# Attention ahead of two expert layers: log series of the softmax sums on GpSimd, a cast and the log's first guess on ScalarE, pair 0 loaded over two queues, some constants set later

## The chip, the cores and the metric

One core of one Trainium2 chip runs one program. The metric is the device time of an execution in microseconds (us); lower is better. The core has TensorE (PE in the rows, its weight loads PEld), VectorE (DVE), ScalarE (ACT), GpSimd (POOL) and SyncE (SP), each with a queue of its own that runs in order, and 16 DMA engines that all queues feed. SP's rows are DMA issues.

## The reference

All inputs are float32. Attention has batch 4, 8 heads, 576 positions, head size 64:

```python
scores = scale * q @ k.T                       # scale = 1/8
cum = np.cumsum(np.log(np.clip(f, 1e-4, 1)), axis=-1)
scores = scores + cum[:, None] - cum[None, :]   # causal: the rest is -1e9
attn = np.exp(scores - max(scores))
attn = attn / (np.sum(attn) + 1e-9)
x = attn @ v                                   # to [2304, 512]
h = x @ w_in; x = np.maximum(0.01 * h, h) @ w_out
```

A layer of 8 experts follows: the tokens are dealt out by gate logits `x @ w_gate`, each expert takes 288 tokens through `max(x @ w1, 0) @ w2`.

## The kernel before, in words

The program has stages: attention (0 to about 213 us), the first half of the dense layer, its second half, the routing with what was deferred, and the experts. The change lies in attention and in constants at the top.

**Attention** runs over 16 pairs of heads. For each pair there are three groups of operations:

- `prepare` (line 606): loads k and q (`load`, `load_end`), transposes them on PE, and splits each into a high part (rounded, on ACT: kh, qh) and a low part (the rest, on DVE: kl, ql). Rows of negated running sums of log f come into `kr` by two DMAs from a DRAM buffer `cumd`.
- `offsets` (line 696): products of q and k with queries on the partitions (four matmuls a block, the last one with `kr`), the mask added and the row maximum taken on DVE (`kept`, `nm`), `exp` with row sums on ACT (`sm`). Then the log of the 10 columns of sums: `guess` (DVE: the float's bits times a constant), `ratio` (ACT: exp of the guess), `series` (DVE: six instructions on 128x10). `rows` (line 675) transposes the result on PE and puts it by two DMAs into the rows of `qr`.
- `attend` (line 788): the products again, now with keys on the partitions and `qr` as a last term, so that `exp` (ACT, into `P`) gives the finished weights; GpSimd zeroes the part above the diagonal; the product with v; `finish` (line 857) splits the result into high and low part (`xt`) and stores it. Half 0 (320 columns) has both parts on DVE, half 1 one on DVE and two steps on GpSimd (`FIN`, line 46).

Buffers: four sets of q/k tiles (`NS`), the set of pairs 0, 4, 8, 12 lies in the tile `X` and shows as X in the rows; four PSUM buffers `s` that all products share. The rows and columns of the sets that products read but no load writes are filled once by GpSimd memsets (`pads`, lines 586 to 600).

**The first expert weights** `wi0` (w_in, unpacked from pairs of 32-bit words) are made beside attention, 16 chunks: three DVE instructions on `wbits`, three GpSimd ones on `wsq` and `wst`, then per 1024 columns two ACT casts and two GpSimd subtractions into `wh`.

**The order.** `Plan` (line 91) is a list scheduler on the host: each operation has an engine, a cost in ns, needs, a rank and buffers; `order` lets each engine take the ready operation of lowest rank. What comes out is the order written into each engine's queue, and it does not change at run time. The ranks of a pair are 12 times its number plus the constants at the top: `ZP` prepare, `ZO` offsets, `ZA` attend, `ZH`/`ZL` high and low part, `ZS` blocks of attend, `ZT`, `ZR` the log, `ZN`/`ZM`/`ZB` offsets by pair; `ZW`, `DW`, `MW` date the weights. `MOVE` is its cost of a DMA.

At the top `make_identity`, the mask, `wgs` (gate weights, by a DMA on SP), `sel` (three DVE adds) and `wg2` are set up before attention; `wgs`, `sel` and `wg2` are first used in the dense stage.

Of the kernel before, what the change touches and what calls it, by code (L numbers as in the profile page):

```python
# [12 lines left out]
FT = mybir.dt.float32  # L13
# [36 lines left out]
NEAR = 11  # L50
NEARB = 5
ZN = 1, 0, 0, 0, 0, 0, 0, 0, 0, 0, 0, 0, 0, 0, 0, 1
ZM = -2.5, -0.5, 0, 0, 0, 0, 0, 0, 0, 0, 0, 0, 0, 0.5, 4, -4
ZB = 0, 0, -4, 0, 0, 0, 0, 0, 0, -2, 0, -4, 0, 0, 0, -1
# [5 lines left out]
PACE = 1.1  # L60

# [29 lines left out]
class Plan:  # L91
# [5 lines left out]
    MOVE = 650, 2200  # L97
# [27 lines left out]
    def order(self):  # L125
# [15 lines left out]
        def start(eng, t):  # L141
            nonlocal form
            q = ready.get(eng)
            while q and free.get(eng, 0) <= t:
# [16 lines left out]
                for b in o.takes:  # L161
                    r = taken[b.ring]
                    k = len(r) - self.depth[b.ring]
                    if k >= 0 and r[k].n:
                        blocked[b.ring].append(o)
                        break
                    if k >= 0 and max(x + self.hop(y, eng) for x, y in r[k].ends) > t:
                        post(max(x + self.hop(y, eng) for x, y in r[k].ends), "arrive", o)
                        break
                else:  # L170
                    for b in o.takes:
                        taken[b.ring].append(b)
# [12 lines left out]
                    free[eng] = t + ns + 25 * (eng == "sp")  # L185
                    done.append(o)
                    post(t + ns, "free", o)
                    if eng == "sp":
# [7 lines left out]
        while events:  # L196
# [3 lines left out]
            elif kind == "end":  # L200
                for u in o.users:
                    u.left -= 1
                    u.at = max(u.at, t + (self.MOVE[1] if o.eng == "sp" else self.hop(o.eng, u.eng)))
                    if not u.left:
                        post(u.at, "arrive", u)
                for b in o.uses:
                    b.n -= 1
                    b.ends.append((t + (self.MOVE[1] if o.eng == "sp" else 0), o.eng))
# [17 lines left out]
def tile_kernel(ctx, tc, q, k, v, f, w_in, w_out, w_gate, w1, w2, out):  # L226
# [14 lines left out]
    for w in WIDE1:  # L241
# [13 lines left out]
    G.affine_select(mask[:, 320:], mask[:, 320:], pattern=[[1, 128]], base=0, channel_multiplier=-1,  # L255
                    compare_op=OP.is_gt, fill=0.0)
# [118 lines left out]
    V.tensor_tensor(sel, sel, ident[:, 64:64 + E], op=OP.add)  # L375
    V.tensor_tensor(sel, sel, ident[:, 96:96 + E], op=OP.add)
    wg2 = cst.tile([128, 2 * NF, 32], FT, name="wg2")
    G.memset(wg2, 0.0)
# [142 lines left out]
    with ExitStack() as c1:  # L521
# [51 lines left out]
        cums = []  # L573
        for l in range(2):
            o = op("vec", 500, lambda l=l: negate(l), [o], -1000, (), [cb])
            cums.append(op("sp", 450, lambda l=l: sp.dma_start(cumd[l], pre["cn"][l].bitcast(FT)), [o], -1000, (), (), 200))
# [10 lines left out]
        for n in range(NS):  # L587
            i = n
            fs = [(560, lambda i=i: gp.memset(QR[i].bitcast(FT), 0.0)), (560, lambda i=i: gp.memset(KR[i].bitcast(FT), 0.0))]
            if n == 0:  # L590
                fs += [(150, lambda: gp.memset(QO.bitcast(FT), 0.0))]
                fs += [(150, lambda u=u: gp.memset(QO[64 * u:64 * u + 2].bitcast(FT), 1.0)) for u in range(2)]
            for u in range(2):
                fs += [(560, lambda i=i, u=u: gp.memset(QR[i][64 * u:64 * u + 2].bitcast(FT), 1.0)),
                       (560, lambda i=i, u=u: gp.memset(KR[i][64 * u + 32:64 * u + 34].bitcast(FT), 1.0))]
            for x, c in ((QH, 0), (QL, 0), (KH, S), (KL, S)):
                fs.append((100, lambda x=x[i], c=c: gp.memset(x[:, c:c + 64].bitcast(FT), 0.0)))
            if n < 2:
                fs.append((150, lambda n=n: gp.memset(VT[n][64:, 4], 0.0)))
            pads.append([op("gp", ns, fn, (), 12 * n - 100) for ns, fn in fs])  # L600


# [3 lines left out]
        def prepare(n, own, z):  # L606
# [5 lines left out]
            loads, buf = {}, {}  # L612

            def load(j, i):
# [4 lines left out]
                sp.dma_start(x3[j][:, :, i], src[b, h + i, :512].rearrange("(t p) d -> p t d", p=128))  # L619

            def load_end(j):
                if j == 0:
                    x3["end"] = at.tile([128, 2, D], FT, name="x4", tag="x4", bufs=2)
                sp.dma_start(x3["end"][64 * j:64 * j + 64], (q if j else k)[b, h:h + 2, 512:].rearrange("h p d -> p h d"))
            for j in range(2):
                o = op("sp", 450, lambda j=j: load(j, 0), (), z - 8, ["x3"], (), 728)
                buf[j] = o.got
                loads[j] = [o, op("sp", 450, lambda j=j: load(j, 1), [], z - 8, (), buf[j], 728)]
            o = op("sp", 625, lambda: load_end(0), (), z - 8, ["x4"], (), 182)
            buf["end"] = o.got  # L630
            loads["end"] = [o, op("sp", 625, lambda: load_end(1), [], z - 8, (), o.got, 182)]
# [38 lines left out]
            for u in range(2):  # L670
                outs[0].append(op("sp", 450, lambda u=u: sp.dma_start(kr[64 * u:64 * u + 2, :S].bitcast(FT), cumd[:, H * b + h + u]),
# [24 lines left out]
        def offsets(n, own, z):  # L696
# [70 lines left out]
            def guess():  # L767
                own["ln"] = x = at.tile([128, 3, 10], FT, name="ln", tag="ln", bufs=2)
                vec.tensor_scalar(x[:, 0], own["sm"].bitcast(I32), LN[0], LN[1], op0=OP.mult, op1=OP.add)

            def ratio():
                act.activation(own["ln"][:, 1], own["ln"][:, 0], AF.Exp)

            def series():
                x, t = own["ln"][:, 2], own["ln"][:, 1]
                vec.scalar_tensor_tensor(t, own["sm"], 1e-9, t, op0=OP.add, op1=OP.mult)
                vec.tensor_scalar(x, t, LN[5], LN[4], op0=OP.mult, op1=OP.add)
                vec.tensor_tensor(x, x, t, op=OP.mult)
                vec.scalar_tensor_tensor(x, x, LN[3], t, op0=OP.add, op1=OP.mult)
                vec.scalar_tensor_tensor(x, x, LN[2], own["ln"][:, 0], op0=OP.add, op1=OP.add)  # L780
                vec.tensor_tensor(x, x, own["nm"][:, :10], op=OP.add)
            o = op("vec", 80, guess, tots, z + ZR, ["ln"], [sb])
            lb = o.got[0]
            p = op("act", 230, ratio, [o], z + ZR, (), [lb])
            o = op("vec", 900, series, [p], z + ZR, (), [nb, sb, lb])
# [122 lines left out]
        run(plan)  # L908
        stp_.__exit__(None, None, None)
# [460 lines left out]
```

## Time and profile before

| | us |
|---|---|
| median of 3 runs (lowest, highest) | 941.02 (940.88, 943.09) |
| the profiled execution | 943.13 |
| its span, first to last instruction | 941.1 |
| PE busy in the span | 893.4 |
| DVE busy | 609.9 |
| ACT busy | 407.2 |
| POOL busy | 438.4 |

The profile is that of one execution. A busy time is the time in which an engine works on an instruction; matmuls are pipelined and their ends modelled, so PE's is rough. "Granted clock" is the share of TensorE's full speed that the chip gave. "x<-y" is what an instruction writes and reads, by tile names. A bracket such as [0.58 <-DVE nm L71] gives the idle time of the engine before an instruction and what ended it. Line L71 is the helper through which all planned operations pass, so rows are told apart by their tiles.

### The profile page before, as it was taken

What the parts mean: (1) busy time and instruction counts of PE and PEld (TensorE: products, weight loads), DVE (VectorE), ACT (ScalarE), POOL (GpSimd) and SP (SyncE); (2) the same over time, 40 slices, a digit from 0 to 9 for tenths busy, and PEclk for the clock granted to TensorE, in tenths of its full rate; (3) what the DMA queues carried; (4) which work ended last, traced back from release to release, by engine and by line L of the source; (5) the groups of instructions that cost most, each with busy time, mean ns of one, the idle gap of its engine ahead of it and who ended that gap; (6) DMA issues with size and microseconds to landing.
All of it is one profiled execution on the core that took longest, in us unless ns stands there. A gap on an engine that the chain in (4) does not pass through costs nothing.

```text
span 941.1 us, 19011 instructions
## 1 busy us (share of the span) xinstructions
PE 893.4 (95%) x6906; PEld 759.8 (81%) x6906; DVE 609.9 (65%) x1552; ACT 407.2 (43%) x949; POOL 438.4 (47%) x548
## 2 busy tenths in 40 slices
PE   6899899999999999999999999999959999999996
PEld 5688787887877887777777777777649999999996
DVE  6899999845789369523466766667735666566631
ACT  5988778861222223312222222123314555555521
POOL 8265666345999149100645655468752122221101
PEclk9999999999999999999899999999889999999998
DMA  5455565369985473521212221121336556556511
GB/s 130 105 156 157 143 161 141 95 196 294 334 298 173 156 222 117 178 90 45 85 62 69 68 68 49 65 68 49 116 126 192 175 187 193 191 185 204 182 41 33
DMA packets 139677, 131.81 MB, mean 140 GB/s; under 512 B 68448, under 2 KB 106656, under 8 KB 139584
## 3 DMA queue, kind: packets, MB, share of 16 engines
q1 hardware_dynamic: 136512, 121.17, 41.8%
q0 software_dynamic: 3072, 9.44, 3.4%
q8 instruction: 54, 0.88, 0.4%
q14 instruction: 39, 0.32, 0.1%
HBM read 99.85 MB, written 30.56 MB: 139 GB/s over the span
## 4 chain that ended last, share of the span: by engine, by line
PE 69%; DVE 11%; issue 11%; POOL 4%; ACT 3%; DMA 1%; POOLq 0%; SPq 0%; ACTq 0%; DVEq 0%
PE acc L1031 21%; PE h L71 21%; PE h L1087 7%; PE s L71 7%; PE y L1100 6%; PE T L71 3%; DVE kept L71 3%; DVE ln L71 3%; PE q_ct L1031 2%; DVE wbits L71 2%; ACT kept L71 2%; POOL out L1108 1%; DVE r_ge L1249 1%; DVE xt L71 1%; PE T L1077 1%
## 5 line engine op out<-in xcount | busy, mean ns | idle before, releaser
L71 PE MATMUL h<-X,wh 128*128 128x512 f32 (+1 forms) x960 | 211.1, 376 | 0.9 <-DVE g L71 0.9
L71 PEld LDWEIGHTS h<-X,wh 128*128 128x128 f32 x960 | 166.1, 189 | 38.4 <-DVE g L71 3.0
L1031 PE MATMUL acc<-wh,gh 128*128 128x512 f32 x576 | 190.3, 406 | 0.0
L461 POOL TENSOR_TENSOR gl<-g,gh 128x512 fp32r<-128x512 f32 x64 | 104.1, 1631 | 75.5 <-ACT gh L460 72.3
L1031 PEld LDWEIGHTS acc<-wh,gh 128*128 128x128 f32 x576 | 108.8, 193 | 19.5
L1087 PE MATMUL h<-XE,wh 128*128 128x288 f32 x768 | 118.3, 303 | 0.3 <-ACT XE L1078 0.3
L71 DVE TENSOR_TENSOR wh<-wst,wh 128x512 fp32r<-128x512 f32 x132 | 90.5, 707 | 42.8 <-ACT wh L360 31.2
L1031 PE MATMUL acc<-wh,gl 128*128 128x512 f32 x288 | 116.9, 406 | 0.0
L360 ACT CAST wh<-wst 128x512 fp32r<-128x512 f32 x132 | 80.4, 621 | 79.9 <-DMA wst<-in_moe_w 47.2
L1087 PEld LDWEIGHTS h<-XE,wh 128*128 128x128 f32 x768 | 106.5, 191 | 0.6 <-ACT XE L1078 0.6
L460 ACT CAST gh<-g 128x512 fp32r<-128x512 f32 x64 | 39.5, 621 | 141.6 <-PE acc L1031 127.1
L71 ACT ACTIVATE g<-h 128x512 f32<-128x512 f32 (+1 forms) x72 | 39.5, 551 | 139.0 <-PE h L71 136.8
L1100 PE MATMUL y<-eh,wh 128*128 128x288 f32 x512 | 98.4, 296 | 0.0
L71 ACT ACTIVATE kept<-kept,nm 128x192 f32<-128x192 f32 (+4 forms) x160 | 87.8, 551 | 17.1 <-DVE nm L71 16.9
L1108 POOL DMA_INDIRECT out<-yo,ids x24 | 24.7, 1028 | 129.3 <-DVE yo L1107 120.1
L1100 PEld LDWEIGHTS y<-eh,wh 128*128 128x128 f32 x512 | 79.5, 188 | 0.2 <-ACT eh L1091 0.2
L71 DVE TENSOR_TENSOR g<-g,h 128x512 f32<-128x512 f32 (+1 forms) x72 | 44.6, 621 | 51.9 <-ACT g L71 51.9
L71 DVE SCALAR_TENSOR_TENSOR wbits<-w,wbits 128x256 int32<-128x256 int32 x128 | 75.3, 589 | 2.8
L71 POOL TENSOR_TENSOR wst<-wsq,wbits 128x256 f32<-128x256 f32 x64 | 49.8, 779 | 46.4 <-DVE wbits L71 42.3
L1100 PE MATMUL y<-el,wh 128*128 128x288 f32 x256 | 67.9, 296 | 0.0
L1031 PEld LDWEIGHTS acc<-wh,gl 128*128 128x128 f32 x288 | 55.4, 192 | 9.8
L71 POOL TENSOR_SCALAR wsq<-wsq 128x256 f32<-128x256 f32 x64 | 59.9, 935 | 5.6
(210 smaller groups left out, 1605.3 us busy)
## 6 DMA issues: line engine op xcount, KB each, us to landing
wst<-in_moe_w SPq DMA_DIRECT2D x128, 256.0 KB
X<-xd SPq DMA_DIRECT2D x12, 1024.0 KB
g<-gd SPq DMA_DIRECT2D x36, 256.0 KB
w<-in_moe_w_in SPq DMA_DIRECT2D x32, 256.0 KB
w<-in_moe_w_out SPq DMA_DIRECT2D x32, 256.0 KB
gd<-g SPq DMA_DIRECT2D x16, 512.0 KB
xd<-xt SPq DMA_DIRECT2D x16, 320.0 KB
x2d<-xo SPq DMA_DIRECT2D x18, 256.0 KB
```

Source lines behind the costliest of these rows:

```text
L71: r = getattr(self.engine, name)(*a, **k)
L360: A.copy(r[u][0], x)
L460: A.copy(gh, g)
L461: G.tensor_tensor(gl, g, gh, op=OP.subtract)
L1031: tc.keep_in_program_order(PE.matmul(*a, **k))
L1077: PE.transpose(p[:, M * t:M * t + M], xe[t][:, 128 * c:128 * c + 128], ident[:M, :M])
L1087: PE.matmul(h[:, :CAP], w, X[:, c, x, :], start=n == 0, stop=n == 3 * NC - 1)
L1100: PE.matmul(yt[c][:, :CAP], w[:, s], a, start=j == 0 and n == 0, stop=j == NJ - 1 and n == 2)
L1108: sd = G.indirect_dma_start(out=out[:, :], out_offset=bass.IndirectOffsetOnAxis(ap=ids[:, 3 * e + t:3 * e + t + 1], axis=0), in_=y, in_off ...
L1249: V.scalar_tensor_tensor(many[:, :NT * (K + 1)].rearrange("p (i k) -> p i k", k=K + 1)[:, :, :K], key[:, :, None].to_broadcast(s), base if ...
```

## The change

- `guess` is dropped on DVE; `ratio` makes it on ACT (copy with scale and bias of the sums' bits) ahead of the exp. The series runs on GpSimd, in nine instructions (`ready` and `series`) in place of six.
- The high part of half 0 is cast on ACT (`FIN`).
- Pair 0: q is loaded from ACT's queue (a planner engine "aq"), its rows of running sums come straight from SBUF (`pre["cn"]`) instead of through `cumd`, and its three `KR` memsets go to DVE. The small pads come before the long ones.
- The mask's triangle, `wgs`, `sel` and `wg2` move back, the last three behind the attention plan.
- Ranks, weight dates, `NEAR` and the planner's DMA cost change.

```diff
-ZP, ZO, ZA, ZH, ZL, ZW, DW = -38, -27, 5, -6, -14.5, 68.5, 15.5
-ZS = 7, 3.5, 7, 1, 3.5, 11.5, 15.5
+ZP, ZO, ZA, ZH, ZL, ZW, DW = -39, -27, 5, -9.5, -10.5, 63, 14.5
+ZS = 5, 5.5, 7, 0.5, 2.5, 11, 11.5
-ZT = -4, 5.5
-ZR = 5
-MW = 2.5, 0.65
+ZT = 0, 7
+ZR = 5.5
+MW = 1.5, 0.6
-FIN = ("vec", "vec"), ("vec", "gp")
+FIN = ("act", "vec"), ("vec", "gp")
-NEAR = 11
+NEAR = 10
...
-    MOVE = 650, 2200
+    MOVE = 650, 2600
...
-    G.affine_select(mask[:, 320:], mask[:, 320:], ...)
...
-    G.memset(wgs, 0.0)
-    with nc.allow_non_contiguous_dma(reason="small"):
-        nc.sync.dma_start(wgs[:, :, :E], w_gate.rearrange("(c p) e -> p c e", p=128))
-    V.tensor_tensor(sel, ident[:, 0:E], ident[:, 32:32 + E], op=OP.add)
...
-    G.memset(wg2, 0.0)
...
+            on = (vec, "vec") if n == 0 else (gp, "gp")
...
+            for x, c in ((KH, S), (KL, S), (QH, 0), (QL, 0)):
                 fs.append((100, lambda x=x[i], c=c: gp.memset(x[:, c:c + 64].bitcast(FT), 0.0)))
+            fs.append((570, lambda i=i: gp.memset(QR[i].bitcast(FT), 0.0)))
+            fs += [(670, lambda i=i, u=u: gp.memset(QR[i][64 * u:64 * u + 2].bitcast(FT), 1.0)) for u in range(2)]
+            ks = [(570, lambda i=i, e=on[0]: e.memset(KR[i].bitcast(FT), 0.0))]
+            ks += [(670, lambda i=i, u=u, e=on[0]: e.memset(KR[i][64 * u + 32:64 * u + 34].bitcast(FT), 1.0)) for u in range(2)]
+            pads.append([op(on[1], ns, fn, (), 12 * n - (100 if n else 1001)) for ns, fn in ks] + [op("gp", ns, fn, (), 12 * n - 100) for ns, fn in fs])
...
+            at_q = (sp, act) if n == 0 else (sp, sp)
+            on = ("sp", "aq") if n == 0 else ("sp", "sp")
...
-                sp.dma_start(x3[j][:, :, i], src[b, h + i, :512].rearrange("(t p) d -> p t d", p=128))
+                at_q[j].dma_start(x3[j][:, :, i], src[b, h + i, :512].rearrange("(t p) d -> p t d", p=128))
...
+                if n == 0:
+                    outs[0].append(op("sp", 450, lambda l=u: sp.dma_start(kr[l:l + 65:64, :S].bitcast(FT), pre["cn"][l][:2].bitcast(FT)), [negs[u]] + pads[0], z + 1, (), [sets[0]], 30))
+                    continue
...
-            def guess():
-                own["ln"] = x = at.tile([128, 3, 10], FT, name="ln", tag="ln", bufs=2)
-                vec.tensor_scalar(x[:, 0], own["sm"].bitcast(I32), LN[0], LN[1], op0=OP.mult, op1=OP.add)
             def ratio():
-                act.activation(own["ln"][:, 1], own["ln"][:, 0], AF.Exp)
+                own["ln"] = x = at.tile([128, 4, 10], FT, name="ln", tag="ln", bufs=2)
+                act.activation(x[:, 0], own["sm"].bitcast(I32), AF.Copy, scale=LN[0], bias=LN[1])
+                act.activation(x[:, 1], x[:, 0], AF.Exp)
+            def ready():
+                x = own["ln"]
+                gp.tensor_scalar(x[:, 3], own["sm"], 1e-9, None, op0=OP.add)
             def series():
                 x, t = own["ln"][:, 2], own["ln"][:, 1]
-                vec.scalar_tensor_tensor(t, own["sm"], 1e-9, t, op0=OP.add, op1=OP.mult)
-                vec.tensor_scalar(x, t, LN[5], LN[4], op0=OP.mult, op1=OP.add)
...
+                gp.tensor_tensor(t, own["ln"][:, 3], t, op=OP.mult)
+                gp.tensor_scalar(x, t, LN[5], LN[4], op0=OP.mult, op1=OP.add)
+                gp.tensor_tensor(x, x, t, op=OP.mult)
+                gp.tensor_scalar(x, x, LN[3], None, op0=OP.add)
+                gp.tensor_tensor(x, x, t, op=OP.mult)
+                gp.tensor_scalar(x, x, LN[2], None, op0=OP.add)
+                gp.tensor_tensor(x, x, own["ln"][:, 0], op=OP.add)
+                gp.tensor_tensor(x, x, own["nm"][:, :10], op=OP.add)
+            o = op("act", 450, ratio, tots, z + ZR, ["ln"], [sb])
+            p = op("gp", 250, ready, tots + [o], z + ZR, (), [sb, lb])
+            o = op("gp", 2200, series, [o, p], z + ZR, (), [nb, sb, lb])
...
         run(plan)
+        G.memset(wgs, 0.0)
+        with nc.allow_non_contiguous_dma(reason="small"):
+            nc.sync.dma_start(wgs[:, :, :E], w_gate.rearrange("(c p) e -> p c e", p=128))
+        V.tensor_tensor(sel, ident[:, 0:E], ident[:, 32:32 + E], op=OP.add)
...
+        G.memset(wg2, 0.0)
```

## Rows read from the trace of the kernel before

**Rows 1.** Stretch view: stretch, length, busy PE, PEld, DVE, ACT, POOL, clock, DMA.
```profile
45.00:165.00 120.00, 110.14 (x1319) 96.47 (x1317) 110.73 (x408) 99.32 (x292) 76.16 (x117) 0.99 0.57 151
```

**Rows 2.** Timeline of PE (start, us): transposed rows, and scores of pair 8.
```profile
55.24 0.27 PE L71 MATMUL s<-ident,ln 128*10 128x128 f32 x1 [0.58 <-DVE nm L71]
...
117.72 0.28 PE L71 MATMUL s<-ident,ln 128*10 128x128 f32 x1 [0.58 <-DVE nm L71]
...
134.47 2.67 PE L71 MATMUL s<-X 64*128 64x320 f32 x32
...
156.39 0.27 PE L71 MATMUL s<-ident,ln 128*10 128x128 f32 x1
...
190.78 0.28 PE L71 MATMUL s<-ident,ln 128*10 128x128 f32 x1
```

**Rows 3.** Waits of PE, 15 to 195 us: total, times, longest.
```profile
PE s L71 <- DVE nm L71: 11.0, 20, 2.0
```

**Rows 4.** Timeline of PE, the longest of these waits.
```profile
142.86 0.40 PE L71 MATMUL s<-kh,qh 64*128 64x288 f32 x2 [1.96 <-DVE nm L71]
```

**Rows 5.** Stretch view just after that wait, columns as in rows 1.
```profile
144.00:146.00 2.00, 1.76 (x8) 1.58 (x9) 2.00 (x14) 2.00 (x7) 1.31 (x3) 0.50 0.00 0
```

**Rows 6.** Timeline of all engines at the front.
```profile
0.79 1.28 ACT L71 ACT_TABLE_LOAD   x1 [0.79 <-PEq L1357]
...
1.25 0.41 SPq L372 DMA_DIRECT2D wgs<-in_moe_w_gate  x1
...
1.71 1.06 SPq L71 DMA_DIRECT2D x<-in_k  x2
...
2.81 1.06 SPq L71 DMA_DIRECT2D x<-in_q  x2
...
3.58 0.68 ACT L71 ACTIVATE ft<-ft 32x576 f32<-32x576 f32 x1 [1.50 <-DVE ft L71]
...
6.42 0.75 DVE L71 SCALAR_TENSOR_TENSOR kept<-cum,kept 32x576 fp32r<-32x576 f32 x1
...
11.17 0.59 SPq L71 DMA_DIRECT2D X<-cumd  x2
...
11.85 0.16 POOL L71 MEMSET kl<- 128x64 f32 x1
...
13.01 0.93 PE L71 MATMUL s<-X,qo 64*128 64x192 f32 x2 [0.18 <-POOL qr L71]
```

**Rows 7.** Stretch view of the ln tile alone: busy PE, PEld, DVE, ACT, clock, DMA.
```profile
0.00:215.00 215.00, 4.50 (x16) 1.36 (x16) 35.54 (x112) 3.34 (x16) 0.98 0.53 142
```

**Rows 8.** The ln tile by instruction: ns min/median/max, 0 to 215 us.
```profile
L71 DVE SCALAR_TENSOR_TENSOR ln<-ln x32: 169/314/1295, 25.2 to 195.9; 128x10 f32<-128x10 f32 x32
```

**Rows 9.** Timeline of DVE and POOL at 112 us.
```profile
111.99 2.54 POOL L71 TENSOR_TENSOR wh<-wst,wh 128x512 fp32r<-128x512 f32 x2
112.01 2.54 DVE L71 SCALAR_TENSOR_TENSOR ln<-ln 128x10 f32<-128x10 f32 x2
```

**Rows 10.** Groups of instructions, POOL, whole span: count | busy us, mean ns.
```profile
L1298 POOL TENSOR_SCALAR r_nr<-r_rp 128x8 f32<-128x8 f32 x7 | 2.2, 319 | 2.4 <-DVE r_rp L1282 2.0
...
L1300 POOL TENSOR_TENSOR r_nr<-r_nr,r_r 128x8 f32<-128x8 f32 x7 | 1.7, 236 | 0.5
```

**Rows 11.** Groups of instructions, ACT, 0 to 215 us.
```profile
L71 ACT CAST kh<-s 128x512 fp32r<-128x512 f32 x12 | 6.8, 564 | 3.4 <-PE s L71 3.4
...
L71 ACT ACTIVATE ln<-ln 128x10 f32<-128x10 f32 x16 | 3.3, 209 | 8.1 <-DVE ln L71 8.1
...
L71 ACT CAST kh<-s 128x64 fp32r<-128x64 f32 x12 | 2.3, 191 | 0.0
```

**Rows 12.** The xt tile by instruction, 0 to 215 us.
```profile
L71 DVE CAST xt<-s x16: 474/479/493, 46.2 to 211.8; 128x320 fp32r<-128x320 f32 x16
```

**Rows 13.** Timeline of SP and POOL at the stage's end.
```profile
213.29 2.99 SPq L71 DMA_DIRECT2D w<-in_moe_w_out  x4
...
215.04 0.74 POOL L71 TENSOR_TENSOR xt<-xt 128x256 fp32r<-128x256 f32 x1
```

More of the change, by code (lines that the diff above doesn't have):

```diff
@@ L49 @@
 WIDE2 = (0,), (1, 2), (3, 4), (5, 6), (7, 8)
-NEAR = 11
+NEAR = 10
 NEARB = 5
-ZN = 1, 0, 0, 0, 0, 0, 0, 0, 0, 0, 0, 0, 0, 0, 0, 1
-ZM = -2.5, -0.5, 0, 0, 0, 0, 0, 0, 0, 0, 0, 0, 0, 0.5, 4, -4
-ZB = 0, 0, -4, 0, 0, 0, 0, 0, 0, -2, 0, -4, 0, 0, 0, -1
+ZN = 0.5, 0, -4, 0, 0, 0, -0.5, 0, 0, 0, 0, 0, 0, 0, 2, 0.5
+ZM = -2.5, -0.5, 0, -1, 0, 0, 0, 0, 0, 0, 0, 1, -1.5, 0.5, 4, -4
+ZB = 0, -4, -5, 0, 0, 0.5, -0.5, 0, 0, -3, 0, -4, 0.5, 0, 0, -1
 NK = 4
@@ L60 @@
 PACE = 1.1
+QS = "sp", "aq"
 class InOrder:
@@ L184, in start @@
                         form = o.form
-                    free[eng] = t + ns + 25 * (eng == "sp")
+                    free[eng] = t + ns + 25 * (eng in QS)
                     done.append(o)
                     post(t + ns, "free", o)
-                    if eng == "sp":
+                    if eng in QS:
                         free["dma"] = max(free.get("dma", 0), t + ns + self.MOVE[0]) + o.move
@@ L202, in order @@
                     u.left -= 1
-                    u.at = max(u.at, t + (self.MOVE[1] if o.eng == "sp" else self.hop(o.eng, u.eng)))
+                    u.at = max(u.at, t + (self.MOVE[1] if o.eng in QS else self.hop(o.eng, u.eng)))
                     if not u.left:
@@ L207, in order @@
                     b.n -= 1
-                    b.ends.append((t + (self.MOVE[1] if o.eng == "sp" else 0), o.eng))
+                    b.ends.append((t + (self.MOVE[1] if o.eng in QS else 0), o.eng))
                     if not b.n:
@@ L254, in tile_kernel @@
     V.memset(mask[:, 320:], -1e9)
-    G.affine_select(mask[:, 320:], mask[:, 320:], pattern=[[1, 128]], base=0, channel_multiplier=-1,
-                    compare_op=OP.is_gt, fill=0.0)
     ones = cst.tile([128, 32], FT, name="ones")
@@ L572, in tile_kernel @@
         cb = o.got[0]
-        cums = []
+        cums, negs = [], []
         for l in range(2):
             o = op("vec", 500, lambda l=l: negate(l), [o], -1000, (), [cb])
+            negs.append(o)
             cums.append(op("sp", 450, lambda l=l: sp.dma_start(cumd[l], pre["cn"][l].bitcast(FT)), [o], -1000, (), (), 200))
@@ L588, in tile_kernel @@
             i = n
-            fs = [(560, lambda i=i: gp.memset(QR[i].bitcast(FT), 0.0)), (560, lambda i=i: gp.memset(KR[i].bitcast(FT), 0.0))]
+            on = (vec, "vec") if n == 0 else (gp, "gp")
+            fs = []
             if n == 0:
                 fs += [(150, lambda: gp.memset(QO.bitcast(FT), 0.0))]
[L592 to L596, printed above, removed]
-                fs.append((100, lambda x=x[i], c=c: gp.memset(x[:, c:c + 64].bitcast(FT), 0.0)))
+                fs += [(220, lambda u=u: gp.memset(QO[64 * u:64 * u + 2].bitcast(FT), 1.0)) for u in range(2)]
+            for x, c in ((KH, S), (KL, S), (QH, 0), (QL, 0)):
+                fs.append((100, lambda x=x[i], c=c: gp.memset(x[:, c:c + 64].bitcast(FT), 0.0)))
+            fs.append((570, lambda i=i: gp.memset(QR[i].bitcast(FT), 0.0)))
[4 more added lines that the diff above has]
+            if n == 0:
+                op("gp", 470, lambda: gp.affine_select(mask[:, 320:], mask[:, 320:], pattern=[[1, 128]], base=0, channel_multiplier=-1,
+                                                       compare_op=OP.is_gt, fill=0.0), (), -99)
             if n < 2:
-                fs.append((150, lambda n=n: gp.memset(VT[n][64:, 4], 0.0)))
-            pads.append([op("gp", ns, fn, (), 12 * n - 100) for ns, fn in fs])
+                op("gp", 150, lambda n=n: gp.memset(VT[n][64:, 4], 0.0), (), 12 * n - 90)
         marks, users = [], []
@@ L623, in load_end @@
                     x3["end"] = at.tile([128, 2, D], FT, name="x4", tag="x4", bufs=2)
-                sp.dma_start(x3["end"][64 * j:64 * j + 64], (q if j else k)[b, h:h + 2, 512:].rearrange("h p d -> p h d"))
+                at_q[j].dma_start(x3["end"][64 * j:64 * j + 64], (q if j else k)[b, h:h + 2, 512:].rearrange("h p d -> p h d"))
             for j in range(2):
-                o = op("sp", 450, lambda j=j: load(j, 0), (), z - 8, ["x3"], (), 728)
+                o = op(on[j], 450, lambda j=j: load(j, 0), (), z - 8, ["x3"], (), 728)
                 buf[j] = o.got
-                loads[j] = [o, op("sp", 450, lambda j=j: load(j, 1), [], z - 8, (), buf[j], 728)]
+                loads[j] = [o, op(on[j], 450, lambda j=j: load(j, 1), [], z - 8, (), buf[j], 728)]
             o = op("sp", 625, lambda: load_end(0), (), z - 8, ["x4"], (), 182)
             buf["end"] = o.got
-            loads["end"] = [o, op("sp", 625, lambda: load_end(1), [], z - 8, (), o.got, 182)]
+            loads["end"] = [o, op(on[1], 625, lambda: load_end(1), [], z - 8, (), o.got, 182)]
             sets = {}
@@ L908, in tile_kernel @@
         run(plan)
+        G.memset(wgs, 0.0)
+        with nc.allow_non_contiguous_dma(reason="small"):
+            nc.sync.dma_start(wgs[:, :, :E], w_gate.rearrange("(c p) e -> p c e", p=128))
+        V.tensor_tensor(sel, ident[:, 0:E], ident[:, 32:32 + E], op=OP.add)
+        V.tensor_tensor(sel, sel, ident[:, 64:64 + E], op=OP.add)
+        V.tensor_tensor(sel, sel, ident[:, 96:96 + E], op=OP.add)
+        G.memset(wg2, 0.0)
         stp_.__exit__(None, None, None)
```

10 lines of the change are left out of this document (1 added, 9 removed).

## The prediction
> **What bounds the kernel now.** The busy times by stretch come first: in the attention stage, from 45 to 165 us, TensorE (PE) is busy 110.14 and VectorE (DVE) 110.73 of 120 us, ScalarE (ACT) 99.32, GpSimd (POOL) 76.16 [rows 1]. Two engines stand at 92%, so an average does not say which one sets the pace. The order of time does: PE transposes the log-sum rows of each head pair once, and the starts of these 16 transpositions are the clock of the stage. From 55.24 to 156.39 us there are 8 intervals of 12.64 us, from 156.39 to 190.78 three of 11.46 [rows 2]. The slow intervals are those in which DVE and POOL also unpack the first expert weights. PE does the same work in both, so 1.18 us of each slow interval is not PE's. The waits say whose it is: between 15 and 195 us PE waited 11.0 us for DVE's row maxima, in 20 waits [rows 3]. One such wait (1.96 us) ends at 142.86 us, and the granted clock from 144 to 146 us is 0.50, the 1.2 GHz level instead of 2.4 [rows 4, 5]; PE had stood idle just before. So DVE's queue sets the slow intervals, and PE the rest.
>
> Before 13 us another chain holds: the first scores need zeroed pads, and the pads end on POOL at about 12.0 us; their last product needs the running sums of f, whose way through DRAM ends at 13.01 us [rows 6].
>
> **The log series leaves DVE.** On DVE the ln instructions take 35.54 us in all, 2.22 us a pair [rows 7]. That is mostly not work: 32 of them have a median of 314 ns and a minimum of 169 [rows 8], and at 112.01 us two took 2.54 us together while POOL ran two weight subtractions over the same 2.54 us [rows 9]. POOL gets nine small instructions a pair instead. The nearest rows are 128x8 ones of the routing stage, 319 ns for a scalar form and 236 for a two-tensor form [rows 10]: four and five of these are 4 x 0.319 + 5 x 0.236 = 2.46 us. POOL has 76.16/120 x 12.64 = 8.02 us an interval now, so 10.5 after. ACT computes the guess: one more instruction like its ln one, 0.21 us [rows 11]. The page "SBUF — State Buffer" of the Trainium skill, section "SBUF: two separate sides", states that DVE and GpSimd share a port pair by an exclusive lock: a DVE instruction with two SBUF inputs and a GpSimd one that reads SBUF do not run together, and the later waits out the earlier. The pair at 112.01 us agrees; it speaks against this change as well, since nine more POOL instructions meet the weight unpacking that stays on DVE. What that would cost is a rival below.
>
> **Half of the rounding leaves DVE.** The 320-wide cast takes 479 ns on DVE [rows 12]. On ACT it lies between the 64- and 512-wide casts, 191 and 564 ns [rows 11]: 0.40 us by width. DVE is relieved by 2.22 + 0.48 = 2.70 us a pair, ACT gets 0.61 more: from 99.32/120 x 12.64 = 10.46 to 11.07 us an interval.
>
> **What this is worth.** With DVE 2.7 us below its 11.66 us an interval (110.73/120 x 12.64), PE's 11.46 is the floor, with ACT at 11.07 and POOL at 10.5 close under it. The bounds of the gain are 0 and 1.18 us an interval; in-order queues this full will not reach the floor, so I take two thirds, 0.8, nearer to the floor because most of PE's waiting is put down to DVE. 8 x 0.8 = 6.4 us. Outside the 8 intervals I take nothing.
> The new guess and series make the chain from sums to rows about 0.45 us longer (2.46 + 0.21 + 0.21 against 2.22 + 0.21). It is covered: the rows transposed at 117.72 us belong to pair 8 (the ninth), whose scores start at 134.47 [rows 2], 16.7 us later. If that cover were gone the price would be 0.45 x 16 = 7 us. What is not covered is PE's own queue: the transposition stands between other PE work, and everything behind it waits when the series is late. The new ranks of the planner (ZS, ZT, ZH, ZL, ZR, the three lists by pair, the weight dates and the longer DMA allowance) cost no instruction; they only move work, and I price them inside the 0 to 1.18.
>
> **The front.** The DMA of the gate weights leaves SP's queue in front of the first k load: issue 0.41 us, so k starts at 1.25 instead of 1.71 us [rows 6]. The q loads of pair 0, issued at 2.81 us now, go to ACT's queue; even behind ACT's table load (0.79 + 1.28 = 2.07 us) they are issued 0.7 us earlier [rows 6]. They cost ACT three issues, ahead of its logarithm of f, before which it waits 1.50 us today [rows 6]. PE's first transpositions move up by about 0.5 us with the loads. On POOL the pads of pair 0 now precede the long memsets, three memsets go to DVE, and the constants go behind the stage; pads then end before 7 us and no longer decide. The running sums are ready on DVE at 6.42 + 0.75 = 7.17 us. Today they go to DRAM and come back: read back from 11.17 us, used at 13.01, 1.84 us from issue to use [rows 6]. Going straight from SBUF, an issue at 7.3 us gives a use at about 9.2. DVE's three memsets of about 0.6 us each fill its idle time ahead of f; should f wait for them, 0.4 us is lost. I take 13.01 - 9.2 - 0.4 = 3.4 us. Bounds: 4.3 if the way is still shorter; 0.5 if the next wait, the loads of pair 1 through the same SP queue, leaves only the wgs issue. If this cover fails the later pairs start as now.
>
> **The end.** The weights' first loads are issued on SP at 213.29 us, and POOL's last attention instruction runs from 215.04 to 215.78 [rows 13]. The gate weights' memset and DMA now stand behind the stage. If they are put in front of those loads, SP adds 0.41 us of issue, and at worst waits for POOL until 215.78: 2.5 us. I take 0.4 and keep 0 to 2.9. The selector's three DVE instructions and the second memset of POOL land in a stretch where both engines wait for these loads.
>
> **Sum.** -6.4 - 3.4 + 0.4 = -9.4 us. The profiled execution took 943.13 us (span 941.1), the median of the three runs is 941.02, 0.2% less; the difference is carried to the median: 931.6 us, given as 931.5.
>
> **Rivals.**
> *Only the front pays.* ACT or PE takes the place of DVE at once: ACT at 11.07 us an interval has to wait for PE and DVE in turn, and the interval stays 12.6. For it: ACT is third at 83% and gets work. Against it: PE's listed waits are for DVE. Time: 941.0 - 3.4 + 0.4 = 938.0 us.
> *The floor is reached.* All 8 intervals go to 11.46 us, the front gives 4.3, and the three intervals before 55.24 us give some 0.5 each: 9.4 + 4.3 + 1.5 = 15.2, so 926 us. For it: DVE would have slack everywhere. Against: ACT and POOL stand within 1 us of PE.
> *Slower: GpSimd delivers the rows late.* The series waits in POOL's queue behind weight work; a block like the one at 111.99 us is 2.54 us long [rows 9]. If it stands behind half such a block in each of the 8 intervals, PE's transposition and all PE work behind it wait 1.27 us: +10.2 us, no relief, -3.4 + 0.4 for front and end: 948 us. It decides once PE waits more than about 1.2 us a pair for POOL. For it: POOL goes to 10.5 of 12.6 us an interval, and the weights' dates are pulled earlier (MW), which packs POOL further. Against it: POOL now waits much of its time, and 16.7 us lie between rows and their use. By the port lock of the Trainium skill's page above, half of the nine instructions waiting out a DVE one of 0.31 us would be an estimated 1.4 us a pair, 941.0 + 8 x 1.4 - 3.0 = 949 us: the same rival by another cause. No row here shows small POOL instructions beside DVE.
>
> **How the numbers follow.** Forecast (927 to 936): 0.47. Only the front (936 to 941): 0.26, a little over half of it below the border. The floor (below 927): 0.13. Slower: 0.14. A measurement of this kernel can tell about 0.3%, 2.8 us, from no change, so faster means below 938.2. Faster 0.47 + 0.13 + 0.14 = 0.74, same 0.12, slower 0.14. The range runs from 924, just past the floor, to 942, which takes in the front case with its worst end (938.0 + 2.5 = 940.5) and leaves out the slower rival.
>
> **What would show it.** Right: the intervals between row transpositions in the weight stretch fall to about 11.8 us, PE's waits for DVE's maxima fall under half of 11.0 us, DVE's busy time there falls below 80% with ACT above 90%, and the product that now waits until 13.01 us goes at 9 to 10. Wrong: PE waits before the row transposition with POOL's ln as releaser (the slower rival); intervals that stay at 12.6 with ACT waited for (only the front); a first product still near 13 us; or w_out loads issued 2 us or more behind the last attention product.

## The result and the profile after

The changed kernel takes 930.4 us (median of 4 runs, 928.31 to 931.35); the kernel before, run beside it, 942.06 (4 runs, 940.88 to 943.10). The ratio is 0.987, 95% interval 0.986 to 0.989. The forecast was 931.5 us with a range of 924 to 942. The profiled execution took 930.69 us, its span 929.0, against 943.13 and 941.1.

The same stretch of the attention stage as in [rows 1]: stretch, length, then busy us (instructions) of PE, PEld, DVE, ACT and POOL, granted clock, DMA share, GB/s.

```profile
45.00:165.00 120.00, 117.55 (x1455) 103.28 (x1451) 87.88 (x355) 113.87 (x339) 97.53 (x219) 1.00 0.59 155
```

DVE fell from 110.73 to 87.88 us, PE rose from 110.14 to 117.55, the clock from 0.99 to 1.00. ACT is at 95% now, POOL at 81%. PE's timeline, the transpositions of the log-sum rows, to be read against [rows 2] (start, length):

```profile
36.33 0.28 PE L72 MATMUL s<-ident,ln 128*10 128x128 f32 x1 [0.55 <-POOL ln L72]
53.74 0.28 PE L72 MATMUL s<-ident,ln 128*10 128x128 f32 x1
...
145.57 0.28 PE L72 MATMUL s<-ident,ln 128*10 128x128 f32 x1
```

The third starts at 36.33 us, the fourth at 53.74, the twelfth at 145.57. The eight intervals between the fourth and the twelfth took 12.64 us each before; now they take (145.57 - 53.74) / 8 = 11.48, which is the pace that PE had before only where no weights were unpacked (11.46). PE's waits, 15 to 195 us (total, times, longest), against [rows 3]:

```profile
PE s L72 <- DVE xr L72: 3.6, 1, 3.6
PE s L72 <- DVE nm L72: 2.2, 6, 1.0
PE s L72 <- POOL P L72: 1.7, 3, 1.3
PE s L72 <- ACT P L72: 1.0, 2, 0.8
PE s L72 <- POOL ln L72: 1.0, 2, 0.6
```

PE's wait for DVE's maxima is 2.2 us, not 11.0; in the eight intervals alone it is 0.2 us, not 7.5. Its waits for POOL's ln are 1.0 us in all 16 pairs, and both of them (at 22.14 and 36.33 us) lie ahead of the eight intervals. One new wait leads the list, 3.6 us for `xr`, once.

The moved work itself, the ln and xt tiles by instruction and form, 0 to 215 us (ns min/median/max of ln; busy us and mean ns of the cast), against [rows 7, 8, 11, 12]:

```profile
L72 POOL TENSOR_TENSOR ln<-ln x64: 202/206/213, 20.3 to 187.3; 128x10 f32<-128x10 f32 x64
L72 POOL TENSOR_SCALAR ln<-ln x48: 204/240/249, 20.6 to 187.0; 128x10 f32<-128x10 f32 x48
L72 POOL TENSOR_SCALAR ln<-sm x16: 241/253/448, 19.6 to 185.2; 128x10 f32<-128x10 f32 x16
L72 ACT ACTIVATE ln<-sm x16: 192/201/213, 19.7 to 184.5; 128x10 f32<-128x10 int32 x16
```

```profile
L72 ACT CAST xt<-s 128x320 fp32r<-128x320 f32 x16 | 6.5, 407 | 5.2 <-PE s L72 5.2
```

What cost DVE 35.54 us costs POOL 32.02 (2.00 us a pair) by the durations shown, and for the two-tensor forms the spread is gone: 202 to 213 ns, where DVE's form of [rows 8] had 169 to 1295.

The front, all engines, against [rows 6]:

```profile
0.93 0.20 POOL L914 MEMSET wgs<- 128x128 f32 x1
1.07 0.53 POOL L920 MEMSET wg<- 128x512 f32 x1
...
3.08 0.59 DVE L72 MEMSET X<- 2x640 f32 x1 [0.17 <-issue]
3.71 0.91 DVE L72 TENSOR_SCALAR ft<-ft 32x576 f32<-32x576 f32 x1
...
7.53 0.74 DVE L72 SCALAR_TENSOR_TENSOR kept<-cum,kept 32x576 fp32r<-32x576 f32 x1
...
8.68 1.22 SPq L72 DMA_DIRECT2D X<-kept  x2
...
11.13 0.36 PE L72 MATMUL s<-X,qo 64*128 64x192 f32 x2 [0.32 <-issue]
```

The first product with running sums starts at 11.13 us, 1.88 earlier than before. On the chip most of "constants later" did not happen: the memsets of lines 914 and 920, written behind the attention plan, still stand at 1 us, and `sel` is done by 4.9 us; of the three constants only the gate weights' DMA moved behind the front, to 21.01 us. So the order of the source lines is not the order of the queues here; the trace does not say why.

The time by stretch of the profiled executions, in us:

| | before | after | difference |
|---|---|---|---|
| start to the fourth transposition | 55.24 | 53.74 | -1.5 |
| fourth to twelfth (8 intervals) | 101.15 | 91.83 | -9.3 |
| twelfth to the first dense product | 57.03 | 57.93 | +0.9 |
| from there to the end of the span | 727.7 | 725.5 | -2.2 |
| span | 941.1 | 929.0 | -12.1 |

The last stretch is not counted for the change: the same PE work stands there in every kernel of this study, and in the fourteen profiles it took 724.6 to 728.3 us, least in e15, which has none of the change. In its first 90 us the granted clock was 0.98 before and 1.00 after. So kernels are compared below by the start of the first dense product as well.

### The profile page after: what moved, and what is told of

It is laid out like the page before. It is cut to its first block, busy times and chain, and to the rows that moved or that the text cites. A ratio compares the mean times of both kernels' runs of the same rounds, so it can differ in the third digit from the quotient of the medians.

```text
span 929.0 us, 19021 instructions
## 1 busy us (share of the span) xinstructions
PE 885.4 (95%) x6906; PEld 751.4 (81%) x6906; DVE 578.2 (62%) x1427; ACT 415.6 (45%) x981; POOL 468.0 (50%) x689
## 4 chain that ended last, share of the span: by engine, by line
PE 69%; issue 11%; POOL 11%; ACT 3%; DVE 3%; DMA 2%; SPq 0%; POOLq 0%; DVEq 0%; ACTq 0%
PE acc L1043 21%; PE h L72 18%; PE s L72 9%; PE h L1099 7%; PE y L1112 7%; PE T L72 3%; POOL wsq L72 3%; ACT kept L72 2%; PE q_ct L1043 2%; POOL wst L72 2%; POOL ln L72 1%; POOL out L1120 1%; DVE r_ge L1261 1%; POOL P L72 1%; DVE kept L72 1%
## 5 line engine op out<-in xcount | busy, mean ns | idle before, releaser
L72 DVE CUSTOM_DVE_ANT_0 kept<-s,mask 128x192 f32<-128x192 f32 (+4 forms) x160 | 59.1, 426 | 23.2 <-PE s L72 22.7
```

The lines of the kernel that those rows point to most:

```text
L72: r = getattr(self.engine, name)(*a, **k)
```

## The experiments

All twelve runs, with the fourth transposition, the mean of the eight intervals and the first dense product in us. Ratios are to the kernel before, run beside them.

| run | median | ratio, 95% | fourth | interval | dense |
|---|---|---|---|---|---|
| before | 942.06 | | 55.24 | 12.64 | 213.42 |
| changed kernel | 930.40 | 0.986 to 0.989 | 53.74 | 11.48 | 203.50 |
| e1 engines, old order | 937.65 | 0.994 to 0.997 | 53.15 | 11.76 | 207.68 |
| e2 order, old engines | 952.29 | 1.009 to 1.015 | 56.65 | 13.49 | 222.11 |
| e3 front alone | 943.09 | 0.999 to 1.003 | 55.82 | 12.86 | 215.83 |
| e6 front undone | 935.44 | 0.991 to 0.996 | 54.44 | 11.68 | 205.43 |
| e9 cast back | 930.96 | 0.984 to 0.992 | 49.91 | 11.81 | 201.94 |
| e15 before, short series | 929.78 | 0.982 to 0.990 | 53.34 | 11.54 | 202.69 |
| e14 after, short series | 925.59 | 0.977 to 0.986 | 49.84 | 11.31 | 198.27 |
| e4 weights' dates old | 932.03 | 0.987 to 0.992 | 51.82 | 11.62 | 203.89 |
| e5 weights later | 931.61 | 0.987 to 0.994 | 49.05 | 11.94 | 203.89 |
| e17 e4 with cast back | 934.46 | 0.986 to 0.993 | 53.73 | 11.73 | 205.20 |
| e12 e5, pads on POOL | 952.44 | 1.009 to 1.016 | 48.82 | 14.38 | 222.71 |
| e18 three loads earlier | 929.22 | 0.985 to 0.988 | 51.05 | 11.62 | 202.00 |

### Engines, order and front, each alone

**e1: the engines without the order.** The kernel before, with `ratio`, `ready`, `series` and `FIN` of the change; ranks, dates and front old.

```diff
-FIN = ("vec", "vec"), ("vec", "gp")
+FIN = ("act", "vec"), ("vec", "gp")
-            o = op("vec", 900, series, [p], z + ZR, (), [nb, sb, lb])
+            o = op("gp", 2200, series, [o, p], z + ZR, (), [nb, sb, lb])
```

> The kernel before with the log series, its guess and the cast on their new engines, all ranks, dates and the front as before. If the relief of VectorE is what pays, the 8 intervals of the weight stretch fall from 12.64 to between 11.5 and 12.0 us and the time to 932 to 937 us against 942 before. If the new order (ranks and dates) pays, the intervals stay above 12.3 and the time lies within 3 us of the kernel before.

Measured 937.65 us. The intervals fell to 11.76 us, PE's waits for DVE's maxima from 11.0 to 4.8 us. The relief of DVE carries the steady gain in the old order too; in that order it was worth 4.2 us (0.45% of the 941.47 run beside it). In the eight intervals PE waited 1.3 us for POOL's ln in this order, and not at all in the changed kernel.

**e2: the order without the engines.** The changed kernel, its front included, with the old `guess`, `series` and `FIN`.

```diff
-FIN = ("act", "vec"), ("vec", "gp")
+FIN = ("vec", "vec"), ("vec", "gp")
-            o = op("gp", 2200, series, [o, p], z + ZR, (), [nb, sb, lb])
+            o = op("vec", 900, series, [p], z + ZR, (), [nb, sb, lb])
```

> The changed kernel with the log series, its guess and the cast back on VectorE; order, dates and front stay new. If the relief of VectorE pays, the intervals of the weight stretch stay at 12.3 us or more and the time is 938 us or more. If the new order pays, the intervals are under 11.8 and the time is under 934 us.

Measured 952.29 us, slower than before. PE's waits in this kernel, 15 to 195 us:

```profile
PE s L72 <- DVE nm L72: 10.9, 14, 2.7
PE s L72 <- POOL P L72: 3.8, 4, 2.8
PE s L72 <- DVE xr L72: 1.9, 2, 1.0
```

DVE is late again (10.9 us), and the granted clock from 45 to 165 us is 0.94. The new ranks and dates do not suit the loaded DVE: with the front, but without the engines, they cost 11 us (1.2%). With the engines, order and front together add about 7 us to what the engines bring (937.65 to 930.40); e6 below divides these 7.

**e3 and e6: the front alone, and the change without it.** e3 is the kernel before with the pads, the queues of pair 0, its direct rows and the constants of the change; e6 is the changed kernel with the old ones.

```diff
-            at_q = (sp, act) if n == 0 else (sp, sp)
-            on = ("sp", "aq") if n == 0 else ("sp", "sp")
...
-                if n == 0:
-                    outs[0].append(op("sp", 450, lambda l=u: sp.dma_start(kr[l:l + 65:64, :S].bitcast(FT), pre["cn"][l][:2].bitcast(FT)), [negs[u]] + pads[0], z + 1, (), [sets[0]], 30))
-                    continue
```

(The core of what e6 takes out, and e3 puts in.)

> The kernel before with the front alone: q of pair 0 from ScalarE's queue, running sums straight from SBUF, pads reordered, constants later. The changed kernel's first product with the running sums went at 11.13 us instead of 13.01; if that carries through, 1.5 to 2.5 us less than before; if the early pairs swallow it, within 1 us of before.

> The changed kernel with the old front (q of pair 0 on SP, sums by way of DRAM, pads and constants as before), all else new. On the old order the front was worth nothing. If it is worth nothing here too, the time is within 2 us of 930.4 and the fourth row transposition starts at 53 to 55 us. If the new order needs it, as forecast (3.4 us), the time is 933 to 935.

In the old order the front is worth nothing in the end: the first product with sums started at 11.08 us and the third transposition at 39.31, 2.9 us earlier than before, but third to fourth then took 16.5 us instead of 13.0, and the fourth started at 55.82, no earlier than before. In the new order, undoing it cost 5.0 us of the median (930.40 to 935.44); 1.9 of that lies ahead of the first dense product (203.50 to 205.43), the rest in the later stages whose spread was told above. Read from the other side, e6 is engines and order without the front: 2.2 us under e1 in the median (935.44 against 937.65; the intervals of the two ratios overlap) and 2.3 at the first dense product. So up to that product order and front add about 2 us each to the engines; the rest of the 7 us is not located.

### What sets the pace

**e15 and e14: the series cut to one addition.** Both keep the order. The shortened series leaves out the polynomial and keeps the last addition, on DVE in e15 (the kernel before), on POOL in e14 (the changed one).

```diff
-                vec.scalar_tensor_tensor(t, own["sm"], 1e-9, t, op0=OP.add, op1=OP.mult)
...
-                vec.tensor_tensor(x, x, own["nm"][:, :10], op=OP.add)
+                vec.tensor_tensor(x, own["ln"][:, 0], own["nm"][:, :10], op=OP.add)
```

> The kernel before with the log series cut to its last addition (the correction of the guess is left out), the planner's costs and so the order unchanged: VectorE loses five of seven ln instructions, and neither ScalarE nor GpSimd gets any. If VectorE's load sets the slow intervals, those of the weight stretch fall from 12.64 to between 11.5 and 12.0 us and the time to 932 to 937 us. If they are set by the order, or by the wait for loads, the time stays within 2 us of 941.5.

> The changed kernel with the series on GpSimd cut to one addition (the correction of the guess is left out), planner's costs and order unchanged: GpSimd loses seven of nine small instructions a pair. If TensorE sets the pace of the weight stretch (busy 102.55 of 105 us), the time is within 2 us of 930.4. If GpSimd's series delivers the rows late, it falls by 3 us or more.

e15 took 929.78 us: five small instructions a pair less on DVE, and nothing else, give as much as the whole change (10.7 us at the first dense product, where the change has 9.9). Its stretch, columns as above:

```profile
45.00:165.00 120.00, 115.75 (x1441) 104.35 (x1439) 102.92 (x392) 108.01 (x321) 79.19 (x124) 1.00 0.60 159
```

With DVE still at 86% the intervals are 11.54 us, and PE's waits for DVE's maxima (15 to 195 us) are 3.3 us instead of 11.0. The cut also shortens the way from the sums to the rows, but PE had no listed wait for `ln` in the kernel before. It was DVE's queue that set the slow intervals.

e14 took 925.59 us, 4.8 under the changed kernel (the intervals of the two ratios just touch); at the first dense product it is 5.2 us. Between the fourth and the twelfth transposition that is 8 x (11.48 - 11.31) = 1.4 us. No wait for ln lies there in the changed kernel, but two for the triangle that POOL zeroes in `P`, 1.4 us together, and e14 has neither. The longer one on POOL and on PE, in the changed kernel:

```profile
121.23 0.21 POOL L72 TENSOR_TENSOR ln<-ln,nm 128x10 f32<-128x10 f32 x1
121.40 2.50 POOL L72 TENSOR_TENSOR wh<-wst,wh 128x512 fp32r<-128x512 f32 x2
123.85 1.74 POOL L72 TENSOR_SCALAR_AFFINE_SELECT P<-P 128x256 f32<-128x256 f32 x5
```

```profile
124.32 2.94 PE L72 MATMUL s<-P,vt 128*64 128x320 f32 x32 [1.28 <-POOL P L72]
```

The series ends at 121.4 us, a block of weight subtractions follows, and only then the triangle that PE waits for. By e14 the series' price in this stage is thus about 1.4 us, and it falls on another tile than ln. The other 3.9 us lie ahead of the fourth transposition (53.74 to 49.84), in the hole that follows: there the weight loads happened to be issued at 32.74 us instead of 34.02, and PE's wait for `xr` was 1.5 us instead of 3.6.

**e9: the cast back on DVE.** The changed kernel with the old `FIN`.

```diff
-FIN = ("act", "vec"), ("vec", "gp")
+FIN = ("vec", "vec"), ("vec", "gp")
```

> The changed kernel with the high part of half 0 cast on VectorE again (0.48 us a pair there, 0.43 less on ScalarE, which is busy 95% of the weight stretch). If VectorE's relief is what pays, most of it is the series and the time is within 2 us of 930.4. If ScalarE is the new bound, 2 us or more faster. If the order needs the cast where it was planned, 2 us or more slower.

Measured 930.96 us: the total does not change, but two parts cancel in it. The intervals are 11.81 us instead of 11.48, 2.7 us in all eight, and PE has waits for DVE's xt that the changed kernel does not have in this stage (15 to 195 us):

```profile
PE s L72 <- DVE xt L72: 2.5, 4, 0.9
```

Against that the fourth transposition started 3.8 us earlier (49.91), without the hole that the next part describes; whether the cast or the planner's other order closed it is not shown.

### The hole behind the third pair

Between the third and the fourth transposition the changed kernel takes 17.4 us; before, it took 13.0 (42.20 to 55.24). DVE's timeline and PE's there (the bracket is idle time and what ended it):

```profile
33.22 0.08 DVE L72 DVE_READ_ACCUMULATOR2_ANT nm<- 128x1 f32 x1
37.17 0.33 DVE L72 TENSOR_SCALAR wbits<-w 128x256 int32<-128x256 int32 x1 [3.86 <-DMA w<-in_moe_w_in]
...
41.11 0.27 DVE L72 TENSOR_TENSOR xr<-s,xr 10x128 fp32r<-10x128 f32 x1
```

```profile
36.76 1.09 PE L72 MATMUL s<-ident,x 128*128 128x128 f32 x8 [0.16 <-ACT P L72]
41.43 5.22 PE L72 MATMUL s<-P,vt 128*64 128x320 f32 x32 [3.58 <-DVE xr L72]
```

The first weight chunk's instruction stands in DVE's queue from 33.3 us, waiting for a load that SP issued at 34.02; the split of the third pair's rows (`xr`) stands behind it. PE is idle for 3.58 us, from 37.85 to 41.43; the granted clock falls in that time and stays at 0.50, the 1.2 GHz level, up to 46 us (the stretch view, columns as above):

```profile
38.00:40.00 2.00, 0.00 (x0) 0.00 (x0) 1.68 (x6) 2.00 (x7) 1.83 (x3) 0.82 0.43 158
40.00:42.00 2.00, 0.57 (x2) 0.30 (x4) 1.96 (x7) 0.42 (x2) 1.83 (x3) 0.50 0.00 0
42.00:44.00 2.00, 2.00 (x16) 1.31 (x14) 1.97 (x6) 0.33 (x2) 0.88 (x2) 0.50 0.42 97
44.00:46.00 2.00, 2.00 (x14) 1.03 (x12) 0.95 (x3) 1.94 (x7) 0.00 (x0) 0.50 0.73 164
```

Four runs try to close it through the planner, one by hand.

**e4, e5, e17, e12: other dates for the weights.**

```diff
-MW = 1.5, 0.6
+MW = 2.5, 0.65
```

(e4; e17 is e4 with the `FIN` of e9.)

> The changed kernel with the old pair numbers that release the weight loads (2.5 + 0.65 a chunk instead of 1.5 + 0.6). The changed kernel's TensorE stands idle from 37.8 to 41.4 us and then runs at half clock to about 46 us, behind weight bits on VectorE whose load was late. If the early date makes that hole, it is gone and the time is 3 to 6 us under the changed kernel (924 to 927). If the hole only moves, or later weights hold up the stage's end, the time stays at 929 to 932.

> The changed kernel with the cast back on VectorE and the weights released at 2.5 + 0.65 a chunk. With the cast back the fourth row transposition already started at 49.9 us and the dense stage 1.6 us earlier than in the changed kernel. If early weight bits on VectorE still cost something there, 925 to 928 us; if TensorE is full anyway, 929 to 932.

```diff
-MW = 1.5, 0.6
+MW = 3.5, 0.55
...
-            on = (vec, "vec") if n == 0 else (gp, "gp")
+            on = (gp, "gp")
```

(e5 is the first of these two, e12 has both.)

> The changed kernel with the weight loads released from pair 3 on (3.5 + 0.55 a chunk). With 2.5 + 0.65 VectorE still stood from 33.2 to 36.4 us behind weight bits whose load had not landed. If those weight bits make the hole before the fourth row transposition, it starts at 48 to 50 us instead of 53.7 and the time is 924 to 927 us. If something else of the front holds pair 3 (its loads through SP), the fourth transposition stays at 52 to 54 us and the time at 929 to 932.

> The weights as in the run with later weights, and pair 0's three long memsets on GpSimd again, so that f's clip does not wait for them on VectorE (3.71 us in the changed kernel, 3.03 before). The first product with the running sums should go at about 10.4 instead of 11.13 us. If the early pairs pass that on, 0.5 to 1 us under the run with later weights; if they swallow it, the same.

None gained. e4 only shortens DVE's wait (3.13 us). In e5 the hole is gone (fourth at 49.05), but the weights then press on the later pairs: the intervals are 11.94 us, PE waits 2.9 us for POOL's ln (1.8 of it at once, at 108.26 us), and the dense product starts at 203.89. e17 shows e4's picture with the hole back (53.73). e12 missed altogether: three memsets of 0.6 us on another engine gave an order with intervals of 14.38 us. The planner answers a small edit with a different order for everything behind it, so these four say little about a single cost.

**e18: three loads earlier, the order of all other engines kept.** The operations that the planner put out are reordered by hand: the first three weight loads go five places up SP's queue.

```diff
-        run(plan)
+        todo = plan.order()
+        early = [o for o in todo if o.eng == "sp" and getattr(o, "got", []) and o.got[0].ring == "w64"][:3]
+        queue = [o for o in todo if o.eng == "sp"]
+        spot = queue.index(early[0])
+        for o in early:
+            todo.remove(o)
+        spot = todo.index(queue[spot - BACK])
+        todo[spot:spot] = early
+        for o in todo:
+            o.fn()
```

> The changed kernel, with the first three loads of the expert weights put five places further up SP's queue (ahead of the k and q loads of pair 3, from 34.0 to about 29.7 us), and nothing else moved: the order on every other engine stays. Theory (the front's gain is lost in one hole, because DVE's in-order queue stands at 33.2 us before a weight chunk that has not come, and two products' input xr stands behind it): DVE's wait of 3.86 us for w_in shrinks below 1 us, PE's wait of 3.58 us for xr below 1 us, the granted clock of 40 to 46 us stays at 1.00, the fourth row transposition moves from 53.74 to about 49.5 us and everything behind it with it; 926 us, ratio to the kernel before near 0.983. Rival (the hole is the price of the series on GpSimd, whose queue stands beside it): the fourth transposition stays at 53 to 54 us, 930 to 931 us. A third outcome: the pair-3 loads, now three issues later, open another hole behind it, and the gain is given back by the end of attention (first dense product at 203 us or later).

Measured 929.22 us. SP's and PE's timeline:

```profile
29.76 3.22 SPq L73 DMA_DIRECT2D w<-in_moe_w_in  x3
```

```profile
27.58 0.41 PE L73 MATMUL s<-kh,qh 64*128 64x288 f32 x2 [1.05 <-DVE nm L73]
...
38.81 0.28 PE L73 MATMUL s<-ident,ln 128*10 128x128 f32 x1 [0.83 <-POOL ln L73]
51.05 0.28 PE L73 MATMUL s<-ident,ln 128*10 128x128 f32 x1
```

With the loads at 29.76 us the waits for w_in and xr are gone, and third to fourth takes 12.2 us instead of 17.4, with the full series on GpSimd. So the hole came from the late load, not from the series. But only 1.5 us of it reach the dense product (203.50 to 202.00): the first three transpositions came 1.4 to 3.1 us later (the first of them, at 25.86 us, before any moved load, so that this much is not the edit's), the granted clock was 0.72 and 0.50 in 28 to 30 and 30 to 32 us instead of 40 to 46, and the interval is 11.62. The time is not told apart from the changed kernel's (the intervals of the ratios overlap), and the 926 us expected were not reached. e18 still has the two waits for POOL's `P` (1.5 us) that e14 does not have; where the rest of e14's lead comes from stays open.

## Why the prediction was right, point by point

**DVE's queue sets the slow intervals: right.** e15 shows it with one cut, e1 with the moved work itself. The stage went as its signs said: waits for maxima 2.2 us (under half of 11.0), DVE at 73% (below 80%), ACT at 95%.

**The steady term: mechanism right, size too small.** The step that failed is "in-order queues this full will not reach the floor, so I take two thirds, 0.8". The intervals fell by 1.16 us, the 1.18 of the upper bound in effect, so 9.3 us instead of 6.4. Nor is 11.46 PE's floor: in e14 the eight intervals average 11.31. Per interval of 11.44 us (the nine up to the thirteenth transposition), DVE now has 87.88 / 120 x 11.44 = 8.4 us, ACT 10.9 (forecast 11.07) and POOL 9.3 (10.5). With ACT at 95% beside it PE kept its pace in the new order; in the old order (e1) the intervals got to 11.76, close to the forecast's 11.8. The new ranks and dates, which I priced inside the 0 to 1.18, are not most of the difference between the two: with them and the old front (e6) the intervals are 11.68. Why they come to 11.48 only together with the new front is not shown.

**The costs of the moved work: right within 0.5 us.** By the durations shown the series is 2.00 us a pair on POOL (2.46 from the routing rows), the guess 0.20 and the cast 0.41 on ACT (0.21 and 0.40). But the nine instructions wait for one another. The start of POOL's timeline in one pair of the weight stretch:

```profile
105.81 0.45 POOL L72 TENSOR_SCALAR ln<-sm 128x10 f32<-128x10 f32 x1
106.34 1.05 POOL L72 TENSOR_SCALAR xt<-xt 128x256 fp32r<-128x256 f32 x1
107.36 0.20 POOL L72 TENSOR_TENSOR ln<-ln 128x10 f32<-128x10 f32 x1
107.65 0.20 POOL L72 TENSOR_SCALAR ln<-ln 128x10 f32<-128x10 f32 x1
107.94 0.21 POOL L72 TENSOR_TENSOR ln<-ln 128x10 f32<-128x10 f32 x1
108.24 0.25 POOL L72 TENSOR_SCALAR ln<-ln 128x10 f32<-128x10 f32 x1
```

The eight of `series` start 0.28 to 0.33 us apart. From the start of `ready` to the end of the last they take 2.64 us in the last two pairs and 3.3 to 3.9 in the weight stretch, where, as here, another operation slips in behind `ready`. The Trainium skill, page "Perfetto Trace Analysis", section "GPSIMD Engine Instruction", advises timing GpSimd instructions by start-to-start spacing and not by the reported duration; the trace agrees, 0.29 against 0.20 us. No wait for ln falls into the eight intervals; the two that came (0.40 and 0.55 us) belong to the first pairs.

**The cast: rightly counted in the 2.7 us relief, but it does not show in the total** (e9). Without its move, with 2.2 us a pair alone, the intervals are 11.81 us; with it 11.48. The missing hole of e9 hides these 2.7 us.

**The front: wrong in size and in what it is worth.** "I take 13.01 - 9.2 - 0.4 = 3.4 us" became 1.88 at the first product. Three parts failed. The clip of f started at 3.71 us, right behind the third DVE memset and 0.68 later than before, and took 0.91 us instead of 0.51; so the second negation started at 7.53 instead of 6.42, and the 0.4 us kept for DVE's memsets was 1.1. The DMA was issued at 8.68 us, behind the writes to `cumd` on the same queue, not right behind the negation (8.27). And from its issue to the use were 2.45 us, not 1.84; by then another input was nearly as late, since PE had waited 0.98 us for the low parts of k and q until 10.23 us. PE's first transposition started at 5.70 us, 0.53 later than before and not 0.5 earlier. The pads had been misread: those of pair 0 lie in X, and the kernel before had written them by 7.43 us (timeline before):

```profile
4.11 3.32 POOL L71 MEMSET X<- 2x640 f32 x8
```

The memsets that ended at 12.0 us belong to another pair's set (`kl`), so pads did not hold the first scores; PE came to them at 11.88 us from transpositions that had waited for a load of q until 10.41. At the third transposition the changed kernel was 5.9 us ahead of the one before (36.33 against 42.20), by front and new order together; the hole behind it took 4.4 of them back, and 1.5 were left at the fourth. e3 puts the front alone at nothing; the rival "only the front pays" falls with it.

**The end: +0.4 us not seen.** The w_out loads were issued at 202.66 us, ahead of the first dense product at 203.50; the memsets and the gate weights' DMA ran long before.

**The slower rival.** GpSimd did not deliver the rows late: 1.0 us of waits for ln in the whole stage, where about 1.2 us a pair would have decided it. Its mechanism, the series packed against a weight block, did appear once, on `P` (1.28 us at 124.32). The port lock of the Trainium skill's page "SBUF — State Buffer", section "SBUF: two separate sides", did not show on POOL's side as feared: two-tensor forms of the series took 202 to 213 ns beside the weight unpacking; the one form that stretched was `ready`, 253 ns in the median and 448 at most. On DVE's side the weight bits still spread from 406 to 972 ns; that this is the lock is not shown.

**The sum.** -6.4 - 3.4 + 0.4 = -9.4 us against -12.1 in the span. The steady term was 2.9 us short and the later stages gave 2.2 us that no step had; the front was 1.9 too much, the last four pairs lost 0.9, and the 0.4 of the end did not come. The errors cancel in part, which is luck, and the forecast was counted from 941.02 us, while the kernel before took 942.06 beside the changed one: the medians fell by 11.7 us, not 9.4. So the forecast's 931.5 us is nearer to 930.4 than its steps deserve, and the mechanism of "the floor is reached" is the one that happened in the eight intervals.

## What to carry to other kernels

Where two engines stand at the same share, take the intervals of a repeating instruction where the extra load is on and where it is off: the difference (12.64 against 11.46 here) is about what a relief can bring, and cutting the suspected load out (e15) tests it. An order made by a list scheduler belongs to its engine loads: the moved work in the old order gave 4 of the 12 us, and the new order and front with the old loads lost 11. A load that leaves one engine can come back as a wait for another tile of its new engine, here `P` instead of ln. A gain at the front counts only where the next wait in an in-order queue, here a load issued at 34 us for an instruction at 33, does not take it back.

## What was not expected of the hardware

Tiny instructions (128x10) are not slower on GpSimd than on DVE in company: medians of 206 to 253 ns by duration, and 0.28 to 0.33 us from start to start, against a median of 314 and up to 1295 ns for DVE's form of [rows 8]. With an idle of 3.58 us on PE came 6 us at the 0.50 clock, the first 1.4 of them still idle; in e18, whose longest wait near there was 1.05 us, a fall of about 4 us still came (28 to 32 us). Of the fourteen profiles, twelve have at least one 2 us stretch at 0.50 to 0.52 between 24 and 46 us, and two have none (e1, e6). Where the hole at 38 us was closed or shortened (e5, e9, e14, e18), a fall stood at 28 to 32 us.
